# Joined output stores, a store queue ordered by evacuation, and constant filler operands in a fused attention + GLU kernel

## Chip, cores, metric

One core of one Trainium2 chip. The metric is the device time of one execution in microseconds (us), as a median over several executions. Every ratio is the mean time of one kernel's fast runs over that of the other's fast runs of the same rounds, so it is not quite the ratio of the medians quoted beside it.

## The reference

Nyström attention (8 batches, 8 heads, 576 rows, head size 64, 32 landmarks), its result as 4608 tokens of 512, then a gated feed-forward layer with 1536 hidden columns:

```python
q_lm = q.reshape(B, H, 32, 18, D).mean(axis=3)      # landmarks: means of 18 rows; k_lm likewise
A, Bm, C = sm(q, k_lm), sm(q_lm, k_lm), sm(q_lm, k)  # sm: scaled softmax
Z = Bm.T / (norm1(Bm) * norminf(Bm))
for _ in range(6):
    Z = 2 * Z - Z @ Bm @ Z
x = (A @ Z @ C @ v)                                 # -> tokens x 512
out = (sigmoid(x @ w_gate) * (x @ w_val)) @ w_out   # fp32, 4608 x 512
```

## The kernel before

The program is ordered while it is built: a model of the engines' times (`Model`) decides which stream of work (loads, landmark sums, Newton steps, feed-forward tiles) emits its next instructions. What the change and the argument touch are the output stores, which go to SyncE's queue, and the things that share this queue: DMA transposes of k and q, and, from batch 3 on, the swap of landmark halves that the product `bs` waits for.

```python
TURN, LATE = 3, 2
PLAIN = min(TURN, LATE)      # batches 0 and 1: rows in permuted order (r, l)
...
# front(b), b >= SWAP (3): two half-swaps of landmark sums, then bq and klm on GpSimd
for what in ("k", "q"):
    s4 = hls[what]
    other[what] = sb.tile([128, H, m], FP32, name=f"s5_{b}{what}", tag="s5", bufs=2)
    for c in range(2):
        nc.sync.dma_start(out=other[what][64 * c:64 * c + 64], in_=s4[64 - 64 * c:128 - 64 * c])
pool.tensor_add(out=klm, in0=hls["k"], in1=other["k"])
...                          # bq likewise, in two halves
# mid(b): the first products of the middle part
mm(out=bs[32 * i:32 * i + 32, g, :], lhsT=bq[0:64, 2 * i + g, 0:m], rhs=klm[0:64, 2 * i + g, :], ...)
...
out3 = out.rearrange("(b p c) n -> b c p n", b=B, c=NC)
out4 = out.rearrange("(b l r c) n -> b c r l n", b=B, r=3, c=NC)
# ffn2(t): a tile of 128 tokens
ob = sb.tile([128, d_model], FP32, name=f"ob_{t}_{x}", tag="ob", bufs=3)[:, 0:w]
...                          # evacuate op to ob on ScalarE or VectorE
r = 0
while r < 128:
    col = 128 * t + r
    bb, y, p0 = col // S, (col % S) // P6, col % P6
    c = 2 * (y % 3) + y // 3
    if bb < PLAIN:
        n, dst = m, out4[bb, c, p0 // m]             # 32 rows
    else:
        n = min(128 - r, P6 - p0)
        dst = out3[bb, c, p0:p0 + n, :]              # 32, 64 or 96 rows
    (nc.scalar if x and r else nc.sync).dma_start(out=dst[:, cs], in_=ob[r:r + n, :])
    r += n
...
def idle(n):                 # filler products
    for _ in range(n):
        mm(out=idle_ps[0][:, 0:256], lhsT=idle_w[:, 0:128], rhs=idle_w, start=True, stop=True)
```

A slice `out4[bb, c, p0 // m]` has 32 rows of 512 numbers. A slice over several `r`, as the change takes it, has the shape 3 x 32 x 512 or 2 x 32 x 512: its slowest dimension is 3 or 2. The source in both cases is a plain piece of `ob` with 96 or 64 partitions.

Of the kernel before, what the change touches and what calls it, by code (L numbers as in the profile page):

```python
# [20 lines left out]
class Model:  # L21
# [73 lines left out]
    def pe(self, out, ins, rows, cols, n, at=(0, 0), slow=0.0):  # L95

        mode = (64 if rows <= 64 else 128, 32 if cols <= 32 else 128)
        beside = mode == self.mode and mode[1] == 32 and at not in self.parts
        drain = 0.0 if mode == self.mode else 0.094
        self.mode = mode  # L100
        self.parts = self.parts | {at} if beside else {at}
        busy = 0.0035 if beside else max(n, 60) / 2400.0 + 0.002 + drain + 0.017 * (cols == 96) + slow
        outs = [out]
        start = self.start("pe", outs, ins)
        self.pass_ticks(start)
        busy = busy if self.warm else 2 * busy
        landed = self.run("pe", outs, ins, busy, 0.2)
        end, columns = start + busy, n * rows / 128.0
        if end > self.TICK * (self.tick + 1):
            rest = columns * (end - self.TICK * (self.tick + 1)) / busy  # L110
            self.columns += columns - rest
            self.pass_ticks(end)
            columns = rest
        self.columns += columns
        return landed

    def pass_ticks(self, t):

        while t >= self.TICK * (self.tick + 1):
            self.warm = self.columns >= 3060  # L120
            self.tick += 1
            self.columns = 0.0

# [11 lines left out]
    def turn(self, src, dst):  # L135

        elements = 1
        for x in src.shape:
            elements *= x
        start = max(self.free["pe"], self.free["sp"], self.landed.get(src.name, 0.0))  # L140
        busy = 0.026 * elements / 2048
        self.free["sp"] = start + busy

        end = self.free["sp"] + (3.0 if self.free["dma"] > start else 2.5)
        self.free["dma"] = max(self.free["dma"], start) + busy
        self.used[src.name] = self.used[dst.name] = self.landed[dst.name] = end
        return end

    def swap(self, src, dst):

        start = max(self.free["pe"], self.free["sp"], self.landed.get(src.name, 0.0))
        self.free["sp"] = start + 0.15
        end = max(self.free["sp"], self.free["dma"]) + 2.5
        self.used[src.name] = self.used[dst.name] = self.landed[dst.name] = end


# [35 lines left out]
def kernel(ctx, tc, q, k, v, moe_w_gate, moe_w_val, moe_w_out, out):  # L192
# [116 lines left out]
        load_w(wo_sb, wo, (slice(None), slice(4 * fc, 4 * fc + 4), slice(None)), ("o", fc))  # L309


    idle_w = consts.tile([128, 256], BF16, name="idle_w")
    nc.vector.memset(idle_w, 1.0)  # L313
    model.free["pool"] = 0.5
    load(0, "k", 2)
    load(0, "q", 2)
# [210 lines left out]
    def mid(b):  # L527
# [117 lines left out]
        yield need(model.landed[Bc.name] + (0.25 if b else 0.0), banks=1)  # L645
        n1 = bank([128, 2, m], FP32, f"n1_{b}")
        mm(out=n1, lhsT=blk, rhs=Bc, start=True, stop=False)
        mm(out=n1, lhsT=eps, rhs=idle_w[:, 0:2 * m], start=False, stop=True)
        ce = sb.tile([128, 2], FP32, name=f"cc_{b}", tag="cc")
        dve.tensor_reduce(out=ce, in_=n1, axis=AX.X, op=ALU.max)  # L650
        rc = sb.tile([128, 2], FP32, name=f"rc_{b}", tag="rc")
# [102 lines left out]

    def calm():

        return model.free["dve"] - 0.3

    def norm(b):

# [169 lines left out]
    def flush():  # L930
        while pending:
            pending.pop(0)()

    def ffn1(b):
# [37 lines left out]
            pending.append(gate)  # L972
        flush()

    out3 = out.rearrange("(b p c) n -> b c p n", b=B, c=NC)
    out4 = out.rearrange("(b l r c) n -> b c r l n", b=B, r=3, c=NC)
    ht_at = []

    def ffn2(t):

        c0 = (128 * t) % (2 * S)
        h = -(-128 * (t + 1) // HF)
        yield lambda: ht_at[h - 1] if halves[0] >= h else None
        if t == 0:
            yield need(*[w_at[("o", fc)] for fc in range(NWC)])

        parts = 2 if t == B * S // 128 - 1 else 1
        w = d_model // parts
        for x in range(parts):
            cs = slice(x * w, x * w + w)  # L990
            yield need(banks=1)
            flush()
            op = bank([128, w], FP32, f"op_{t}_{x}", True)
            for j in range(NFC):
                mm(out=op, lhsT=ht[:, j, c0:c0 + 128], rhs=wo_sb[:, j, cs],
                   start=(j == 0), stop=(j == NFC - 1))
                if j % 2 == 1 and j < NFC - 1:
                    yield need()
                    flush()
            ob = sb.tile([128, d_model], FP32, name=f"ob_{t}_{x}", tag="ob", bufs=3)[:, 0:w]  # L1000
            if x == 1:
                dve.tensor_scalar_mul(out=ob[:, 0:w // 2], in0=op[:, 0:w // 2], scalar1=0.5)
                act.mul(out=ob[:, w // 2:], in_=op[:, w // 2:], mul=0.5)
            elif model.free["act"] + 0.1 < model.free["dve"]:
                act.mul(out=ob, in_=op, mul=0.5)
            else:
                dve.tensor_scalar_mul(out=ob, in0=op, scalar1=0.5)
            done_with(op)
            r = 0
            while r < 128:  # L1010
                col = 128 * t + r
                bb, y, p0 = col // S, (col % S) // P6, col % P6
                c = 2 * (y % 3) + y // 3
                if bb < PLAIN:
                    n, dst = m, out4[bb, c, p0 // m]
                else:
                    n = min(128 - r, P6 - p0)
                    dst = out3[bb, c, p0:p0 + n, :]
                (nc.scalar if x and r else nc.sync).dma_start(out=dst[:, cs], in_=ob[r:r + n, :])
                r += n  # L1020
        tiles[0] = t + 1


# [68 lines left out]
    def ffn1s():  # L1092
        for b in range(B):
            yield from ffn1(b)
# [7 lines left out]
    def idle(n):  # L1102

        if not idle_ps:
            idle_ps.append(bank([128, d_model], FP32, "idle_ps"))
        for _ in range(n):
            mm(out=idle_ps[0][:, 0:256], lhsT=idle_w[:, 0:128], rhs=idle_w, start=True, stop=True)

    def due(x):

# [7 lines left out]
    def weave(sides, main1, main2):  # L1118
# [9 lines left out]
                (mains if x in mains else streams).remove(x)  # L1128

        while streams or mains:  # L1130
            now = model.free["pe"] + SLACK
            best, least, held = None, None, False
            tiled = model.mode[1] == 32
            first = list(mains)
            if len(mains) == 2 and 27 * 24 * B * count[1] < 24 * 27 * B * (count[0] - LAG):
                first.reverse()
            elif len(mains) == 2 and max(model.free["dve"], model.free["act"]) > model.free["pe"] + BEHIND:
                first.reverse()
            if tiled:
                for x in streams + first:  # L1140
                    if not callable(x[0]) and x[0][2] is not None and due(x[0])[1] <= now:
                        best = x
                        break
            for x in streams + first if best is None else ():
                data, t = due(x[0])
                if data is None:
                    continue
                if not callable(x[0]) and x[0][2] and not tiled:

                    if x[2] is None and t <= now:  # L1150
                        x[2] = now
                    if x[2] is None or now < x[2] + x[0][2]:
                        if x[2] is None:
                            least = least if least is not None and least[0] <= t + 0.01 else (t + 0.01, x)
                        continue
                banks = not callable(x[0]) and x[0][1] > 0
                if t <= now and not (banks and held):
                    best = x
                    break
                if data <= now:  # L1160
                    held = held or banks
                if t < Model.NEVER and (least is None or t < least[0]):
                    least = (t, x)
            if best is None:
                best = least[1] if least is not None else next(x for x in streams if x[2] is not None)
                least = least or (now, best)
                if halves[0] == 0 and least[0] > now:
                    idle(int(FILL * (least[0] - now) / (0.107 if model.warm else 0.214)))
            if best in mains and not callable(best[0]):
                count[0 if best[1] is main1 else 1] += 1  # L1170
            model.free["pe"] = max(model.free["pe"], due(best[0])[1])
            advance(best)

    SLACK, LAG, FILL, BEHIND = 0.02, 20, 1.0, 1.2
    model.free["pe"] = 1.0
    idle(21)
    weave([loads(), first_squares(), newtons(), norms(), values(), mids(), lands(), fronts()], ffn1s(), ffn2s())


# [28 lines left out]
```

## Time and profile before

| | before |
|---|---|
| time, median | 269.49 us (268.86 to 270.08) |
| span of the profiled run | 268.0 us |
| TensorE busy | 260.6 us, 97% |
| TensorE waits for bq (batch 3) | 0.9 + 0.5 us |
| loads of k and q, issue to landing (median) | 7.9 and 11.0 us |

The stretches, waits and SyncE's queue are shown in the prediction. Some more lines matter later. The first is the granted TensorE clock in 40 slices of the span, in tenths (9 is full). The second is SyncE's DMA queue: packets, megabytes, share of 16 engines' time. Then come the loads of k and q, with their median time to landing.

```profile
PEclk9999999999999999999999999999999999999998
...
q1 hardware_dynamic: 38896, 18.52, 33.8%
...
kn<-in_k_dram POOLq DMA_DIRECT2D x7, 576.0 KB, 7.9
qn<-in_q_dram POOLq DMA_DIRECT2D x7, 576.0 KB, 11.0
```

Last, TensorE's waits for bq over the whole run (sum, number of waits, longest), and a stretch (DMA share: the last number but one):

```profile
PE bs L263 <- POOL bq L167: 0.9, 1, 0.9
PE sl L263 <- POOL bq L167: 0.5, 1, 0.5
...
85.00:100.00 15.00, 13.73 (x197) 7.62 (x198) 10.39 (x30) 10.63 (x31) 2.18 (x3) 1.00 0.94 150
```

SyncE's queue has 38896 packets. 2256 of these have 4 bytes. I read them as completions, one from each DMA engine that a transfer uses: two stores that run alone have 32 of them (the view is in the prediction), and the one store in ScalarE's queue, of 96 rows, has 112 packets, 96 and 16. The trace does not name the engine of a packet. By this reading the number of packets tells how many engines the stores used.

### The profile page before, as it was taken

The page shows a single profiled execution, that of the slowest core. Times are in us where ns is not written, and L with a number is a line of the kernel's source. Part 1 is how long each engine was busy: PE and PEld are TensorE (multiplying, and loading weights), DVE is VectorE, ACT ScalarE, POOL GpSimd, SP SyncE. Part 2 cuts the span into 40 slices and gives each one's busy share as a digit, 9 for nine tenths or more (in the row PEclk, how much of TensorE's full clock was granted, in tenths as well). Part 3 has the DMA queues.
Part 4 walks back from the last instruction along what each step waited for, and adds up shares of the span by engine and source line. Part 5 has one row for each costly group of instructions (what it writes and reads, how often), then busy time and mean ns, then how long its engine had stood idle before and what let it go on. Part 6 is the DMA issues. An engine that isn't in the chain of part 4 may idle for free.

```text
span 268.0 us, 8085 instructions
## 1 busy us (share of the span) xinstructions
PE 260.6 (97%) x3110; PEld 164.0 (61%) x3110; DVE 206.2 (77%) x617; ACT 161.1 (60%) x412; POOL 96.0 (36%) x107
## 2 busy tenths in 40 slices
PE   8999999999998999999999999999999999999994
PEld 6877867756663466546673666546663666557543
DVE  4578789966896679888997579877898689879611
ACT  3676876856544765687456774376746764378401
POOL 8522324950594009630692219530583000000000
PEclk9999999999999999999999999999999999999998
DMA  6999999999897998959996998959913340220134
GB/s 93 183 205 204 207 206 206 205 203 169 171 162 155 170 167 154 218 93 188 168 157 141 149 183 150 237 95 190 181 41 81 80 100 2 68 53 0 42 91 106
DMA packets 62646, 38.01 MB, mean 142 GB/s; under 512 B 33552, under 2 KB 58128, under 8 KB 62608
## 3 DMA queue, kind: packets, MB, share of 16 engines
q0 software_dynamic: 23600, 18.88, 47.0%
q1 hardware_dynamic: 38896, 18.52, 33.8%
q8 instruction: 24, 0.39, 0.6%
q14 instruction: 14, 0.11, 0.1%
q10 hardware_dynamic: 112, 0.10, 0.1%
HBM read 37.75 MB, written 9.44 MB: 176 GB/s over the span
## 4 chain that ended last, share of the span: by engine, by line
PE 89%; POOL 3%; DVE 2%; ACT 2%; DMA 1%; issue 1%; ACTq 0%; DVEq 0%; POOLq 0%
PE op L263 33%; PE gp L263 17%; PE vp L263 16%; PE idle_ps L263 4%; POOL s_3q L167 2%; DMA s_3q<-s_3q 1%; PE cv L263 1%; PE pn L263 1%; PE sc L263 1%; PE tp_k L268 1%; PE rb L263 1%; PE tp_q L268 1%; PE sa L263 1%; PE up_2g L263 1%; PE up_1g L263 1%; PE up_0g L263 1%
## 5 line engine op out<-in xcount | busy, mean ns | idle before, releaser
L263 PE MATMUL op<-wo_sb,ht 128*128 128x512 bf16 (+1 forms) x444 | 110.6, 374 | 0.0
L167 ACT ACTIVATE th<-gp 128x288 bf16<-128x288 f32 x192 | 77.1, 414 | 42.3 <-PE gp L263 33.9
L167 DVE SCALAR_TENSOR_TENSOR ht<-th,vp 128x288 bf16<-128x288 bf16 x192 | 81.1, 448 | 16.0 <-ACT th L167 12.0
L263 PE MATMUL vp<-an,V 128*128 128x288 bf16 x384 | 78.6, 286 | 0.1
L263 PE MATMUL gp<-an,U 128*128 128x288 bf16 x384 | 78.5, 286 | 0.0
L263 PEld LDWEIGHTS <-ht 128*128 128x128 bf16 x444 | 37.4, 98 | 32.5 <-issue 7.5
L263 PEld LDWEIGHTS <-U 128*128 128x128 bf16 x384 | 36.0, 98 | 20.7 <-issue 0.8
L263 PEld LDWEIGHTS <-V 128*128 128x128 bf16 x384 | 37.5, 98 | 10.0 <-DVE V L167 0.3
L167 ACT ACTIVATE ob<-op 128x512 f32<-128x512 f32 (+1 forms) x28 | 16.5, 588 | 30.9 <-PE op L263 28.1
L167 DVE TENSOR_SCALAR ob<-op 128x512 f32<-128x512 f32 (+2 forms) x10 | 6.2, 624 | 13.7 <-PE op L263 13.5
L167 DVE TENSOR_TENSOR an<-aexp,rb 128x384 bf16<-128x384 bf16 (+1 forms) x32 | 13.7, 451 | 1.7 <-PE rb L263 1.4
L167 DVE SCALAR_TENSOR_TENSOR sy<-sy,pn 128x192 bf16<-128x192 bf16 (+1 forms) x35 | 13.3, 381 | 1.0
L263 PE MATMUL idle_ps<-idle_w 128*128 128x256 bf16 x66 | 12.0, 320 | 1.2 <-DVE idle_w L313 1.2
L167 DVE TENSOR_TENSOR sd<-blk,pn 128x256 bf16<-128x256 bf16 x30 | 12.4, 414 | 0.0
L167 ACT ACTIVATE aexp<-sa 128x288 bf16<-128x288 f32 x32 | 10.8, 417 | 1.4 <-PE sa L263 0.7
L263 PEld LDWEIGHTS <-sel 80*128 80x128 bf16 x80 | 6.3, 98 | 5.3 <-issue 0.8
L263 PEld LDWEIGHTS <-WT 64*32 64x32 bf16 x384 | 3.8, 89 | 9.4 <-issue 8.0
L167 ACT CAST U<-up_0g 128x512 bf16<-128x512 f32 x8 | 4.7, 585 | 7.5 <-PE up_0g L263 7.5
L263 PE MATMUL pn<-sy,sd 128*128 128x96 bf16 (+1 forms) x72 | 8.8, 204 | 0.0
L263 PEld LDWEIGHTS <-idle_w 128*128 128x128 bf16 x66 | 6.9, 114 | 3.0 <-DVE idle_w L313 1.2
L286 POOL DMA_DIRECT2D kn<-in_k_dram x9 | 7.0, 783 | 4.7 <-ACT aexp L167 2.2
L167 ACT ACTIVATE cl<-sl 128x288 bf16<-128x288 f32 x20 | 8.0, 409 | 1.0 <-PE sl L263 0.7
(207 smaller groups left out, 374.9 us busy)
## 6 DMA issues: line engine op xcount, KB each, us to landing
vn<-in_v_dram POOLq DMA_DIRECT2D x8, 576.0 KB, 9.0
kn<-in_k_dram POOLq DMA_DIRECT2D x7, 576.0 KB, 7.9
qn<-in_q_dram POOLq DMA_DIRECT2D x7, 576.0 KB, 11.0
out_dram<-ob SPq DMA_DIRECT2D x53, 64.0 KB, 3.0
out_dram<-ob SPq DMA_DIRECT2D x17, 192.0 KB, 2.3
out_dram<-ob SPq DMA_DIRECT2D x18, 128.0 KB, 2.5
wg_sb<-in_moe_w_gate_dram POOLq DMA_DIRECT2D x3, 512.0 KB, 21.2
wv_sb<-in_moe_w_val_dram POOLq DMA_DIRECT2D x3, 512.0 KB, 21.6
```

What stands on the lines that cost most here:

```text
L167: f(**kw)
L263: nc.tensor.matmul(**kw)
L268: nc.tensor.transpose(**kw)
L286: nc.gpsimd.dma_start(out=t[:, hs], in_=src[b, hs].rearrange("h (p c) d -> p h (c d)", p=P6))
```

## The change

Its intent: less issue time on SyncE (36 stores of 32 rows become 18, mostly of 96 or 64), stores that enter SyncE's queue only when their tile is evacuated so that they do not block transposes and swaps behind them, and fillers that start without waiting for a VectorE memset. The model's constants are re-fitted with it, which moves some instructions. The core of the diff:

```diff
-    idle_w = consts.tile([128, 256], BF16, name="idle_w")
-    nc.vector.memset(idle_w, 1.0)
+    ones = nc.const_aps.tensor(1.0, [128, 256], BF16)
 ...   (Model: clock, swap, transposes and stores timed anew; cut)
+    def put_out(keep):
+        while stores and (len(stores) > keep or stores[0][0] <= model.free["pe"]):
+            stores.pop(0)[1]()
 ...
+            put_out(2)
             ob = sb.tile([128, d_model], FP32, name=f"ob_{t}_{x}", tag="ob", bufs=3)[:, 0:w]
 ...
-                if bb < PLAIN:
-                    n, dst = m, out4[bb, c, p0 // m]
-                else:
+            def store(x=x, cs=cs, ob=ob, at=at):
 ...
                     n = min(128 - r, P6 - p0)
-                    dst = out3[bb, c, p0:p0 + n, :]
-                (nc.scalar if x and r else nc.sync).dma_start(out=dst[:, cs], in_=ob[r:r + n, :])
+                    if bb < PLAIN:
+                        dst = out4[bb, c, p0 // m:(p0 + n) // m]
+                    else:
+                        dst = out3[bb, c, p0:p0 + n, :]
+                    (nc.scalar if x and r else nc.sync).dma_start(out=dst[..., cs], in_=ob[r:r + n, :])
 ...
+            stores.append((at, store))
 ...
-            mm(out=idle_ps[0][:, 0:256], lhsT=idle_w[:, 0:128], rhs=idle_w, start=True, stop=True)
+            mm(out=idle_ps[0][:, 0:256], lhsT=ones[:, 0:128], rhs=ones, start=True, stop=True)
 ...
-    model.free["pe"] = 1.0
-    idle(21)
+    model.free["pe"] = 0.6
+    idle(22)
```

More of the change, by code (lines that the diff above doesn't have):

```diff
@@ L101, in pe @@
         self.parts = self.parts | {at} if beside else {at}
-        busy = 0.0035 if beside else max(n, 60) / 2400.0 + 0.002 + drain + 0.017 * (cols == 96) + slow
         outs = [out]
@@ L105, in pe @@
         self.pass_ticks(start)
-        busy = busy if self.warm else 2 * busy
+        each = n if self.warm else 2 * n
+        busy = 0.0035 if beside else max(each, 60) / 2400.0 + 0.002 + drain + 0.017 * (cols == 96) + slow
         landed = self.run("pe", outs, ins, busy, 0.2)
         end, columns = start + busy, n * rows / 128.0
-        if end > self.TICK * (self.tick + 1):
-            rest = columns * (end - self.TICK * (self.tick + 1)) / busy
+        if end > (self.TICK * (self.tick + 1) - 1.2):
+            rest = columns * (end - (self.TICK * (self.tick + 1) - 1.2)) / busy
             self.columns += columns - rest
@@ L117, in pass_ticks @@
     def pass_ticks(self, t):
-        while t >= self.TICK * (self.tick + 1):
-            self.warm = self.columns >= 3060
+        while t >= (self.TICK * (self.tick + 1) - 1.2):
+            self.warm = self.columns >= (3060 if self.warm else 3700)
             self.tick += 1
@@ L137, in turn @@
         elements = 1
-        for x in src.shape:
+        for x in src.shape[1:]:
             elements *= x
         start = max(self.free["pe"], self.free["sp"], self.landed.get(src.name, 0.0))
-        busy = 0.026 * elements / 2048
-        self.free["sp"] = start + busy
-        end = self.free["sp"] + (3.0 if self.free["dma"] > start else 2.5)
+        loading = self.loads[-1] + 1.0 > start
+        busy = 0.0011 * elements * (1.2 if loading else 1.0)
+        self.free["sp"] = start + busy + 0.1
+        end = self.free["sp"] + (3.6 if loading else 2.2)
         self.free["dma"] = max(self.free["dma"], start) + busy
@@ L147, in turn, with store @@
         return end
+    def store(self, t, n):
+        self.free["sp"] = max(self.free["sp"], t) + 0.45 * n
     def swap(self, src, dst):
         start = max(self.free["pe"], self.free["sp"], self.landed.get(src.name, 0.0))
-        self.free["sp"] = start + 0.15
-        end = max(self.free["sp"], self.free["dma"]) + 2.5
+        self.free["sp"] = start + 1.1
+        end = max(self.free["sp"] + (2.4 if self.loads[-1] > start - 3.0 else 1.0), self.loads[-1] + 2.5)
         self.used[src.name] = self.used[dst.name] = self.landed[dst.name] = end
@@ L647, in mid @@
         mm(out=n1, lhsT=blk, rhs=Bc, start=True, stop=False)
-        mm(out=n1, lhsT=eps, rhs=idle_w[:, 0:2 * m], start=False, stop=True)
+        mm(out=n1, lhsT=eps, rhs=ones[:, 0:2 * m], start=False, stop=True)
         ce = sb.tile([128, 2], FP32, name=f"cc_{b}", tag="cc")
@@ L755, in calm @@
     def calm():
-        return model.free["dve"] - 0.3
+        return model.free["dve"] - 1.0
     def norm(b):
@@ L973, in ffn1 @@
         flush()
+    stores = []
+    def put_out(keep):
+        while stores and (len(stores) > keep or stores[0][0] <= model.free["pe"]):
+            stores.pop(0)[1]()
     out3 = out.rearrange("(b p c) n -> b c p n", b=B, c=NC)
@@ L1002, in ffn2 @@
                 dve.tensor_scalar_mul(out=ob[:, 0:w // 2], in0=op[:, 0:w // 2], scalar1=0.5)
-                act.mul(out=ob[:, w // 2:], in_=op[:, w // 2:], mul=0.5)
+                at = act.mul(out=ob[:, w // 2:], in_=op[:, w // 2:], mul=0.5)
             elif model.free["act"] + 0.1 < model.free["dve"]:
-                act.mul(out=ob, in_=op, mul=0.5)
+                at = act.mul(out=ob, in_=op, mul=0.5)
             else:
-                dve.tensor_scalar_mul(out=ob, in0=op, scalar1=0.5)
+                at = dve.tensor_scalar_mul(out=ob, in0=op, scalar1=0.5)
             done_with(op)
-            r = 0
-            while r < 128:
-                col = 128 * t + r
-                bb, y, p0 = col // S, (col % S) // P6, col % P6
-                c = 2 * (y % 3) + y // 3
-                if bb < PLAIN:
-                    n, dst = m, out4[bb, c, p0 // m]
-                else:
-                    n = min(128 - r, P6 - p0)
-                    dst = out3[bb, c, p0:p0 + n, :]
-                (nc.scalar if x and r else nc.sync).dma_start(out=dst[:, cs], in_=ob[r:r + n, :])
-                r += n
+            def store(x=x, cs=cs, ob=ob, at=at):
+                r = k = 0
+                while r < 128:
+                    col = 128 * t + r
+                    bb, y, p0 = col // S, (col % S) // P6, col % P6
+                    c = 2 * (y % 3) + y // 3
+                    n = min(128 - r, P6 - p0)
+                    if bb < PLAIN:
[3 more added lines that the diff above has]
+                    (nc.scalar if x and r else nc.sync).dma_start(out=dst[..., cs], in_=ob[r:r + n, :])
+                    r, k = r + n, k + 1
+                model.store(at, k)
+            stores.append((at, store))
         tiles[0] = t + 1
@@ L1130, in weave @@
         while streams or mains:
+            put_out(3)
             now = model.free["pe"] + SLACK
@@ L1174 @@
     SLACK, LAG, FILL, BEHIND = 0.02, 20, 1.0, 1.2
-    model.free["pe"] = 1.0
-    idle(21)
+    model.free["pe"] = 0.6
+    idle(22)
     weave([loads(), first_squares(), newtons(), norms(), values(), mids(), lands(), fronts()], ffn1s(), ffn2s())
+    put_out(0)
 _INS = ['q', 'k', 'v', 'moe_w_gate', 'moe_w_val', 'moe_w_out']
```

## The prediction

In it, k is the number of DMA engines that one transfer uses. The trace of before shows 16 completions for each of two stores, in the view that is quoted. That the joined stores use 3 or 2 engines was my assumption from their shapes; no trace had shown a k below 16. Two of its figures can be read from the starts of products in the same trace: the fillers start 0.213 us apart at first and 0.109 apart from 9.15 us on, and a change of mode takes 0.09 us (two products op at 117.38 us take 0.52 to the start of the tiled bs, two at 116.46 take 0.43 to the start of a gp).

> **What bounds the kernel now.** I read the page first, then busy time by stretches of 10 us, then the instructions around the one hole that these show, and last the queue of SyncE (SP) and its transfers.
>
> ```profile
> PE 260.6 (97%) x3110; PEld 164.0 (61%) x3110; DVE 206.2 (77%) x617; ACT 161.1 (60%) x412; POOL 96.0 (36%) x107
> ```
>
> TensorE (PE) is busy 260.6 of 268.0 us, so 7.4 us can be won at most from its idle time. The stretches say where that is:
>
> ```profile
> 0.00:10.00 10.00, 8.47 (x104) 6.72 (x105) 4.84 (x21) 4.34 (x7) 7.91 (x15) 1.00 0.83 117
> ...
> 80.00:90.00 10.00, 8.67 (x105) 3.95 (x111) 6.71 (x18) 5.55 (x16) 3.79 (x6) 1.00 0.74 140
> 90.00:100.00 10.00, 10.00 (x147) 6.21 (x145) 7.44 (x25) 7.39 (x22) 0.00 (x0) 1.00 1.13 183
> ...
> 260.00:270.00 10.00, 4.20 (x32) 2.84 (x30) 0.85 (x3) 0.87 (x2) 0.00 (x0) 0.83 0.32 80
> ```
>
> The second number is PE's busy time in the stretch: 1.5 us idle at the start, 1.3 in 80 to 90, some 0.6 over 10 to 50, 3.8 in the tail (268.0 less 264.2), none elsewhere. Before 50 us PE is also padded with filler products (idle_ps, 66 of them, 12.0 us). In 80 to 90 the wait is for GpSimd (POOL), and behind that for a small transfer which SyncE issues. The view of waits for 83 to 88 us, and the chain there:
>
> ```profile
> PEld L263 <- POOL bq L167: 2.0, 2, 1.4
> POOL klm L167 <- DMA s_3k<-s_3k: 1.7, 1, 1.7
> POOL bq L167 <- DMA s_3q<-s_3q: 1.6, 1, 1.6
> ...
> 80.98 3.93 DMA s_3q<-s_3q
> ```
>
> bs, the first product of batch 3's middle part, needs bq, which needs two half-swaps of landmark sums (s_3k, s_3q). These are behind the output stores in the same SyncE queue:
>
> ```profile
> 58.63 1.78 SPq L1019 DMA_DIRECT2D out_dram<-ob  x4
> 60.54 4.83 SPq L400 DMA_TRANSPOSE kT<-kn  x1
> 65.48 3.96 SPq L400 DMA_TRANSPOSE qT<-qn  x1
> 69.49 5.17 SPq L1019 DMA_DIRECT2D out_dram<-ob  x8
> 76.07 1.18 SPq L498 DMA_DIRECT2D s_3k<-s_3k  x2
> 77.39 1.89 SPq L1019 DMA_DIRECT2D out_dram<-ob  x4
> 80.98 1.11 SPq L498 DMA_DIRECT2D s_3q<-s_3q  x2
> ```
>
> Four stores of 32 rows cost 1.78 us of issue, 0.45 each. From their start the transposes take nine and six us to land.
>
> [...] The trace agrees for the stores of before: in 251.5 to 254.3 us only two of them run, 128 rows of 2 KB:
>
> ```profile
> DMA packets 160, 0.26 MB, mean 94 GB/s; under 512 B 32, under 2 KB 32, under 8 KB 160
> ...
> q1 hardware_dynamic: 160, 0.26, 32.6%
> ```
>
> 128 large packets and 32 small ones: 16 completions for each store. [...] the first 21 fillers take 4.66 us (0.22 each), those at 9.15 us six in 0.82.
>
> **The change part by part.** The order of the built programs is the other source. PE's order is the same up to batch 2's last third (some 100 us) but for fillers; bs of batch 3 has not moved.
>
> *Fillers.* The memset of idle_w (0.27 us on VectorE) goes, and its constant is written by GpSimd at 0.31 us. PE's first product, at 1.19 us for want of idle_w, can come where the other engines start, 0.74 to 0.86: 0.35 us earlier. But the first real product (5.65) waits for a load that lands at 5.5, and load issue does not change, so those 0.35 us are filled, not won: the program has 23 fillers there for 21, 0.43 us at 0.213. It also has 4 for 3 before the next group and 11 for 6 before the first of q. Six more at 0.108 are 0.65 us. Before, PE finished those fillers near 9.81 and the q data let it go on at 9.96, so 0.15 is absorbed. I expect PE 0.4 to 0.5 us late from there; later loads land 0.3 to 1.3 us before use, so they hide none of it.
>
> *Stores joined.* Batches 0 and 1 are nine tiles of 128 rows, 36 stores before. After, each group of three tiles has 2 stores of 3x32 rows, 2 of 32 and 2 of 2x32: 18 in all, 18 x 0.45 = 8 us less issue time. Two fewer stand ahead of kT of batch 3: 0.9 us. If the bytes go as before, its chain (transposes, 11 us of GpSimd sums, swap, bq) comes 0.9 us sooner, and the hole shrinks from about 1.65 us (from 84.56 to 86.61, less the 0.4 of work in it) to some 0.3, since PE itself comes 0.45 later. Then the net is +0.45 -1.35 = -0.9.
>
> *Order of stores.* From batch 4 on SyncE's queue changes little (stores of tile 10 go behind the transposes instead of ahead). Those waits are off PE's path: PE shows 10.00 of 10.00 there.
>
> *Order on PE from 100 us on.* Normalisation products move forward; mode changes between tiled and whole products go from 103 to 101, at 0.09 us: -0.2. Tail and number of real products: unchanged.
>
> Sum if the DMA side is harmless: 269.5 - 0.9 - 0.2 + 0.2 (new small waits) = 268.6.
>
> **The rivals.** *First: the joined stores use few DMA engines.* Their destination has a slowest dimension of 3 or 2, the source 96 or 64 rows[...]. On the busiest engine three tiles then put 34 + 64 + 34 = 132 packets, before 8 + 8 + 8 = 24. One 2 KB packet takes, in the lines above, 32.6% x 2.8 us x 16 / 128 = 0.11 us. Nine tiles: 396 x 0.11 = 45 us of packet time against 8, so 37 more. From 55 to 116 us the loads' queue is busy 50.9% and SyncE's 50.0% of 16 engines, 62 us of packet time in 61. With 37 more a busy engine has 98 in 61; packets overlap (the DMA share reached 1.31), so the capacity is about 80 and 18 do not fit. [...] In detail for batch 3: ob_0's 34 packets stand before kT (26 more x 0.11 = +2.9, part of it in its slack), then ob_1 and ob_2 put 98 instead of 16 before the swap of s_3k (82 x 0.11 = 9), ob_3 another 26 before s_3q; some 3 us of all that falls into idle time. bq would come 7 to 10 us later and PE wait 8 to 10 at bs. Batch 4 has the same (tiles 6 to 8) with the slack of 2 us that I see in before (s_4q lands at 115.1, bs at 117.9): 3 to 6 more. Sum: +12, 281, with 274 to 285 possible. For it: [...] the swap is already behind in the queue. Against: nothing in this trace shows it; the program might be lowered otherwise; and someone who measured would hardly have kept a store that costs 4%.
>
> *Second: all is hidden or eaten.* The hole of batch 3 closes by as much as the fillers cost, and the time stays at 269.5. For it: the order up to there is unchanged and PE is full everywhere else.
>
> *Third: the clock.* [...] The loads absorb most of it: 0 to -0.4.
>
> **Range and chances.** I give the few-engine case a good third[...]; of that, most is over 2% (5.4 us). The rest lies between 268 and 270. Faster by over 2% would need 264.1, more than the hole, the start and the mode changes together (about 2.3 us). The point, 271.5, is between the two cases and nearer the likelier; 267.6 is the best of the first sum, 282 the bulk of the rival.
>
> **What would show it.** Packets of q1 (38896 before): with 18 stores fewer at 16 completions each, 38608; with k of 3 and 2 on twelve of them, 38446. Landing of joined stores: 2 to 6 us, or 8 and more for those of tiles 1 and 2. The wait of PE for bq in 80 to 100: under 1 us, or 6 and more; swap s_3q landing at about 84.5, or after 91. Fillers: 74, the group of 11 ending after 10.3 us with no wait for q behind it. The main error would be a k that the chip does not use; next, new waits in PE's changed order after 100 us, which I take as nothing.

## The result

| | before | after |
|---|---|---|
| time, median of 6 runs | 269.14 us | 290.53 us (289.83 to 291.68) |
| ratio | | 1.0794 (95%: 1.0765 to 1.0824), slower |
| span of the profiled run | 268.0 us | 288.0 us |
| TensorE busy / idle | 260.6 / 7.4 us | 265.2 / 22.8 us |

The page of the changed kernel, in the order of the lines shown of before: busy times, clock, SyncE's queue, the chain that ended last by engine, and the loads.

```profile
PE 265.2 (92%) x3118; PEld 165.2 (57%) x3118; DVE 205.9 (71%) x616; ACT 161.2 (56%) x412; POOL 96.0 (33%) x107
...
PEclk9999999999995799996899999999999999999999
...
q1 hardware_dynamic: 38446, 18.52, 30.8%
...
PE 70%; DMA 14%; POOL 8%; DVE 3%; ACT 2%; issue 1%; POOLq 0%; DVEq 0%; ACTq 0%
...
kn<-in_k_dram POOLq DMA_DIRECT2D x7, 576.0 KB, 14.5
qn<-in_q_dram POOLq DMA_DIRECT2D x7, 576.0 KB, 18.9
```

SyncE's queue has 38446 packets, the very number that the prediction gave for k of 3 and 2; 1806 of them have 4 bytes, 450 fewer than before. Transfers that the change does not touch land later: q takes 18.9 us instead of 11.0. DMA has 14% of the chain that ended last, where it had 1%, and the clock has two dips.

Where TensorE stands is seen in the same stretches as before (stretch, its length, then busy time and instruction counts of PE, PEld, DVE, ACT and POOL, granted clock, DMA share, GB/s):

```profile
80.00:90.00 10.00, 5.08 (x48) 2.65 (x46) 5.22 (x15) 3.31 (x7) 1.23 (x2) 0.86 0.58 119
90.00:100.00 10.00, 6.96 (x72) 2.35 (x73) 2.79 (x5) 3.83 (x13) 2.24 (x3) 0.62 0.55 99
```

Before had 8.67 and 10.00 us of PE here, at full clock. What PE waits for between 83 and 96 us (sum, number of waits, longest), and the transfer at the end of it in the chain (start, duration):

```profile
PE bs L268 <- POOL bq L172: 7.6, 1, 7.6
...
POOL bq L172 <- DMA s_3q<-s_3q: 5.5, 1, 5.5
```
```profile
80.53 11.28 DMA s_3q<-s_3q
```

The swap s_3q was issued at 80.53 us, 0.45 earlier than before, and took 11.28 us instead of 3.93. SyncE did not hold it up; its queue around it:

```profile
70.18 2.59 SPq L1033 DMA_DIRECT2D out_dram<-ob  x4
75.64 1.71 SPq L502 DMA_DIRECT2D s_3k<-s_3k  x2
77.52 1.71 SPq L1033 DMA_DIRECT2D out_dram<-ob  x2
80.53 1.13 SPq L502 DMA_DIRECT2D s_3q<-s_3q  x2
```

Four stores where there were eight, two where there were four: their issue time fell from 7.06 to 4.30 us, though by less than half. The swap was no later in the queue. It was slow after its issue. What the DMA engines did meanwhile stands in two stretches that lie wholly inside TensorE's two waits:

```profile
86.00:91.50 5.50, 0.00 (x0) 0.00 (x0) 0.45 (x2) 0.00 (x0) 0.42 (x1) 0.62 0.20 48
128.60:133.80 5.20, 0.00 (x0) 0.00 (x0) 0.00 (x0) 0.00 (x0) 0.57 (x1) 0.79 0.14 37
```

The DMA share is 0.20 and 0.14 of 16 engines: that is the work of 3.2 and 2.2 engines on average while the swap and TensorE waited. In 85 to 100 us of before the share was 0.94.

In batch 4 the same happens again. The chain has the swap s_4q there:

```profile
121.11 13.04 DMA s_4q<-s_4q
```

Before, the swaps of s_4q landed 3.3 to 3.6 us after issue. TensorE waits 8.6 us for bq there. The clock record shows half rate from 87.28 to 97.52 and from 131.66 to 138.48 us: the clock drops within each wait, and the work after it starts at half speed. In PE's timeline the first work after the first wait is:

```profile
92.72 0.24 PE L268 MATMUL bs<-klm,bq 64*32 64x32 bf16 x8 [7.64 <-POOL bq L172]
...
93.88 2.74 PE L268 MATMUL op<-wo_sb,ht 128*128 128x512 bf16 x6
```

These six products took 1.47 us before, and 2.74 now.

The 20.0 us between the two spans are accounted for: TensorE's idle time grew by 15.4 us, its busy time by 4.6. Its waits for bq grew from 1.4 us (0.9 + 0.5) to 16.8 (16.2 + 0.6), which is the 15.4:

```profile
PE bs L268 <- POOL bq L172: 16.2, 2, 8.6
PE sl L268 <- POOL bq L172: 0.6, 2, 0.3
```

Of the 4.6, the eight additional fillers are 1.1 (13.1 less 12.0); the other 3.5 are the same products, slower.

### The profile page after: what moved, and what is told of

Same layout as the page of the kernel before. It is cut to its first block, busy times and chain, and to the rows that moved or that the text cites.

```text
span 288.0 us, 8077 instructions
## 1 busy us (share of the span) xinstructions
PE 265.2 (92%) x3118; PEld 165.2 (57%) x3118; DVE 205.9 (71%) x616; ACT 161.2 (56%) x412; POOL 96.0 (33%) x107
## 3 DMA queue, kind: packets, MB, share of 16 engines
q1 hardware_dynamic: 38446, 18.52, 30.8%
## 4 chain that ended last, share of the span: by engine, by line
PE 70%; DMA 14%; POOL 8%; DVE 3%; ACT 2%; issue 1%; POOLq 0%; DVEq 0%; ACTq 0%
PE op L268 26%; PE gp L268 13%; PE vp L268 12%; DMA kT<-kn 6%; DMA s_4q<-s_4q 5%; DMA s_3q<-s_3q 4%; PE idle_ps L268 4%; POOL s_4k L172 2%; POOL s_4q L172 2%; POOL s_3q L172 2%; POOL s_3k L172 1%; PE pn L268 1%; PE tp_k L273 1%; PE tp_q L273 1%; PE cv L268 1%
## 5 line engine op out<-in xcount | busy, mean ns | idle before, releaser
L268 PE MATMUL op<-wo_sb,ht 128*128 128x512 bf16 (+1 forms) x444 | 112.3, 379 | 0.0
L172 ACT ACTIVATE th<-gp 128x288 bf16<-128x288 f32 x192 | 77.4, 414 | 42.8 <-PE gp L268 34.0
L172 DVE SCALAR_TENSOR_TENSOR ht<-th,vp 128x288 bf16<-128x288 bf16 x192 | 82.6, 449 | 25.8 <-PE vp L268 12.1
L268 PEld LDWEIGHTS <-ht 128*128 128x128 bf16 x444 | 38.7, 99 | 33.6 <-issue 7.9
L172 ACT ACTIVATE ob<-op 128x512 f32<-128x512 f32 (+1 forms) x28 | 16.4, 586 | 30.3 <-PE op L268 24.6
L172 DVE TENSOR_SCALAR ob<-op 128x512 f32<-128x512 f32 (+2 forms) x10 | 6.3, 625 | 24.1 <-PE op L268 23.9
L268 PE MATMUL bs<-klm,bq 64*32 64x32 bf16 x64 | 1.8, 183 | 16.2 <-POOL bq L172 16.2
L172 DVE SCALAR_TENSOR_TENSOR sy<-sy,pn 128x192 bf16<-128x192 bf16 (+1 forms) x35 | 13.3, 381 | 1.0
L268 PE MATMUL idle_ps<-const-bfloat16-1.0 128*128 128x256 bf16 x74 | 13.1, 316 | 0.9 <-PEq L1211 0.8
L268 PEld LDWEIGHTS <-bq 64*32 64x32 bf16 x144 | 1.8, 95 | 20.8 <-POOL bq L172 18.5
L172 DVE TENSOR_TENSOR an<-aexp,rb 128x384 bf16<-128x384 bf16 (+1 forms) x32 | 13.0, 447 | 0.0
L172 DVE TENSOR_TENSOR sd<-blk,pn 128x256 bf16<-128x256 bf16 x30 | 12.4, 415 | 0.0
L172 ACT ACTIVATE aexp<-sa 128x288 bf16<-128x288 f32 x32 | 10.8, 417 | 1.6 <-PE sa L268 0.9
L172 ACT ACTIVATE E<-bs 128x64 f32<-128x64 f32 x8 | 1.8, 224 | 15.0 <-PE bs L268 15.0
L268 PEld LDWEIGHTS <-const-bfloat16-1.0 128*128 128x128 bf16 x74 | 7.8, 114 | 3.1 <-issue 1.3
L268 PEld LDWEIGHTS <-sd 128*128 128x128 bf16 x72 | 6.2, 97 | 4.9 <-DVE sd L172 1.4
## 6 DMA issues: line engine op xcount, KB each, us to landing
qn<-in_q_dram POOLq DMA_DIRECT2D x7, 576.0 KB, 18.9
```

Of the source, the lines that this page charges most:

```text
L172: f(**kw)
L268: nc.tensor.matmul(**kw)
```

## The experiments

The theory after the result, which the packets (38446) and the DMA share in the waits (0.20 and 0.14 of 16 engines) suggest but no trace shows engine by engine: the joined stores run on 3 or 2 DMA engines, these get 16 engines' work to do, and a transfer that also uses the others finishes with them. The rivals: the delay comes from the new order of stores in the queue, from longer stores ahead of the swap (size or position), or from another part of the change.

**The change without the joining, and the joining without the change.** First the changed kernel with its 32-row stores kept:

```diff
                     if bb < PLAIN:
-                        dst = out4[bb, c, p0 // m:(p0 + n) // m]
+                        n = m
+                        dst = out4[bb, c, p0 // m]
```

> The change without its joining: stores of 32 rows for batches 0 and 1, all else as in the changed kernel. If the few DMA engines of the joined stores (k of 3 and 2) are the cause: 268 to 270 us, PE's wait for bq of batch 3 some 1 to 2 us and of batch 4 none, q1 back to about 38896 packets. If the new order of the stores in SyncE's queue or of the products on PE is the cause: still 280 us or more, with the waits for bq where they are.

Measured: 270.03 us against 269.45 of before, ratio 1.0007 (0.9978 to 1.0037). The queue has 38896 packets again, and no wait for bq shows in the trace, in batch 3 or 4 (in batch 3 I had expected 1 to 2 us). Then the kernel before, with nothing but the joining:

```diff
-                    n, dst = m, out4[bb, c, p0 // m]
+                    n = min(128 - r, P6 - p0)
+                    dst = out4[bb, c, p0 // m:(p0 + n) // m]
 ...
-    ....dma_start(out=dst[:, cs], in_=ob[r:r + n, :])
+    ....dma_start(out=dst[..., cs], in_=ob[r:r + n, :])
```

> The kernel before with its 32-row stores joined and nothing else. Few engines: 288 to 292 us, waits of 7 to 9 us for bq of batches 3 and 4, q1 at 38446 packets. Order of stores or products: 268 to 270 us.

Measured: 290.43 us, ratio 1.0754 (1.0693 to 1.0815). PE's waits of this kernel:

```profile
PE bs L263 <- POOL bq L167: 16.1, 2, 8.6
```

The joining alone makes the whole loss, with the same two waits; order, fillers and model add nothing that the runs resolve.

**Number of engines, with bytes and number of stores held the same.** The changed kernel with natural row order in batches 0 and 1 (`PLAIN = 0`) can cut its stores anywhere. One version cuts each run of 96 rows into 93 + 3 and each of 64 into 62 + 2; the other into 80 + 16 and 48 + 16. Both have 30 stores there and the same bytes. I took the first to use 3 and 2 engines and the second 16; the packets below are the test of that.

```diff
-    PLAIN = min(TURN, LATE)
+    PLAIN = 0
 ...
                     n = min(128 - r, P6 - p0)
+                    if bb < 2:
+                        n = {96: 93, 64: 62}.get(n, n)     # e8;  e9: {96: 80, 64: 48}
```

> The change with batches 0 and 1 in natural row order (destination a plain run of rows), and each run of 96 rows stored as 93 + 3, each of 64 as 62 + 2[...]. Twin of the next run, with the same number of stores, 30, and the same bytes. Few engines: near the changed kernel, 286 to 295 us. Rival, that the shape with an outer 3 or 2 or the size of a joined store (192 KB in one) is what costs, and not k: 268 to 271.

> As the run before it, but cut as 80 + 16 and 48 + 16 rows, so that k is 16 for every store. Few engines: 268 to 270 us. If the size of the stores or the row order costs: as its twin.

Measured: 289.22 us for 93 + 3, ratio 1.0715 (1.0652 to 1.0779), and 269.12 us for 80 + 16, ratio 0.998 (0.996 to 1.0). The queue line and the waits for bq of the first, then the queue line of the second, whose trace has no such wait:

```profile
q1 hardware_dynamic: 38476, 18.52, 31.1%
```
```profile
PE bs L268 <- POOL bq L172: 14.0, 2, 7.6
```
```profile
q1 hardware_dynamic: 38800, 18.52, 32.6%
```

This is the cleanest pair. No 3-dimensional destination is left in either kernel, the stores are plain rows, and moving the cut by 13 or 14 rows costs 20 us. The packets fit these numbers of engines: against 36 stores of 16 completions (576 in 38896), 6 x (3 + 3) + 6 x (2 + 2) + 6 x 16 = 156 give 38476, and 30 x 16 = 480 give 38800.

**Fewer stores on all engines.** The intent of the joining, without its shape: natural rows, 96 and 64 rows in one store each.

```diff
-    PLAIN = min(TURN, LATE)
+    PLAIN = 0
```

> The change with batches 0 and 1 in natural row order, so that joined stores have 96 or 64 plain rows on both sides: 18 joined stores as in the change, k of 16. Few engines: 268 to 269.5 us, at or a little under the kernel before, with the wait for bq of batch 3 shorter than its 1.6 us because two issues fewer stand before the transposes. Size of stores: 280 or more.

Measured: 269.62 against 269.38 us, ratio 0.9998 (0.9974 to 1.0022), with 38608 packets, the count for 18 stores of 16 completions. Its trace shows no wait for bq: the hole of batch 3 is closed, as the change intended. The span of that trace is 267.4 us, 0.6 less than before, and the timed runs do not resolve even that. So the intended gain is at most 0.7 us by the interval. In the traces the six op products behind the hole start 1.23 us earlier than before (85.63 against 86.86), but the end comes only 0.6 earlier: about half of the gain is lost again after the hole. Where was not found.

**Where the delay arises.** The stores joined in batch 0 only (tiles 0 to 4), then in batch 1 only (tiles 4 to 8):

```diff
                     n = min(128 - r, P6 - p0)
+                    if bb == 1:        # e4;  e10: bb == 0
+                        n = m
```

> The change with stores joined in batch 0 alone (tiles 0 to 4), 32 rows in batch 1 (tiles 4 to 8). Few engines: the wait before bs of batch 3 stays 5 to 8 us (most of the stores ahead of its swaps are batch 0's), that of batch 4 goes under 1 us; time some 276 to 279. If the two waits depended on one common backlog that only builds up over all nine tiles, both would shrink by a like share.

> The counterpart of e4: the changed kernel with the stores joined in batch 1 only (batch 0 keeps its 32-row stores). Theory (few DMA engines, local to the stores in flight): PE does not wait for bq of batch 3, waits 8 to 10 us at bs of batch 4 and then loses 1.5 to 2 us to the halved clock: 279 to 282 us, and the two halves together (e4 +9.6) make up the whole +21. SyncE's packets 38896 - 225 = 38671, as in e4. Rival (batch 4's wait is a backlog that batch 0's stores began and batch 1's only prolong): the wait of batch 4 is under 5 us and the time under 277.

Measured: 278.97 us for batch 0 (ratio 1.0356), 284.31 us for batch 1 (ratio 1.0521; 281.38 to 285.54 in four runs). Batch 0's stores make the wait of batch 3 (7.5 us) and none in batch 4; those of batch 1 make the wait of batch 4 and none for bq in batch 3. PE's waits of the second:

```profile
PE bs L268 <- POOL bq L172: 9.1, 1, 9.1
PE cv L268 <- DMA ct<-cl: 2.8, 1, 2.8
```

So each wait belongs to the stores that are under way at its swap, and batch 4's is no backlog of batch 0. The two excesses, +9.6 and +15.1, are more than the whole (+20.6): with batch 1 alone a wait of 2.8 us for the transposes ct of batch 3 appears, which is absent from the changed kernel; there PE comes later to that place, which may be why. It halved the clock too, as the granted clock of the stretch behind it shows (0.50):

```profile
101.20:103.00 1.80, 1.43 (x50) 1.11 (x52) 0.87 (x3) 0.00 (x0) 0.00 (x0) 0.50 1.21 262
```

My expectation of 279 to 282 missed that wait.

**Queue or engines.** The joined stores issued from ScalarE, so that they are not in one queue with transposes and swaps:

```diff
-    (nc.scalar if x and r else nc.sync).dma_start(...)
+    (nc.scalar if (x and r) or (bb < PLAIN and n > m) else nc.sync).dma_start(...)
```

> The change with the joined stores issued from ScalarE's queue instead of SyncE's. If the swaps are late because they stand behind the stores' descriptors in one queue of the busy engines: the swap of s_3q lands within 5 us of its issue and the waits for bq fall to 1 to 4 us, 272 to 278 in all. If the busy engines' capacity is the limit, whatever the queue: waits stay 6 to 9 us, 285 or more. ScalarE also pays 12 issues of some 0.6 us.

Measured: 289.89 us, ratio 1.0747 (1.0699 to 1.0796), no better. Of the issues on ScalarE, for which I had expected 0.6 us, one took 0.74 (at 106.99 us) and two 2.24 (at 114.06). Two of PE's waits:

```profile
PE bs L268 <- POOL bq L172: 9.4, 1, 9.4
PE pn L268 <- ACT th L172: 6.1, 1, 6.1
```

The swap s_3q took only 4.85 us here, but the transpose qT of the same batch 18.11 us, and the loads of k and q for batch 4 took 18.8 and 21.3 us. The second wait has another immediate cause: ScalarE stood 7.4 us (the view of its waits: `ACT th L172 <- DMA qT<-qn: 7.4, 1, 7.4`) at the issue of a joined store until the transpose qT, 16.11 us long, had landed. So the equal total is in part a cost of issuing from ScalarE, and only batch 3 is a clean comparison. There, freed from the queue, the delay moved to the earlier transfer of the same chain. That speaks against the idea that only the order within SyncE's queue matters.

**The clock.** Fillers into the accumulator bank of bs, ahead of bs in batches 3 and 4: first 60 and 60, then 64 and 76, to cover the idle time that the first version left (0.7 and 1.8 us).

```diff
+        for _ in range({3: 64, 4: 76}.get(b, 0)):           # e11;  e6: 60 in each
+            nc.tensor.matmul(out=whole[:, 0:256], lhsT=ones[:, 0:128], rhs=ones, start=True, stop=True)
         for g in range(2):                                  # the bs products follow
```

> The change with 60 filler products (6.5 us) ahead of bs in batches 3 and 4, in the time in which PE waits. They do not shorten the wait, but keep the clock up. If PE's halved clock after each wait is a cost of its own, the time falls by 3 to 4 us to 286 to 288 and no 0.5 stands in the granted clock after the waits. If that cost is nothing: no change, or a little slower.

> e6 with more fillers: 64 ahead of bs in batch 3 and 76 in batch 4, to cover the 0.7 and 1.8 us of idle time that e6 left there. Theory (the halved clock after the two waits costs some 3.5 us): the clock stays full after both, and the time is 3 to 4 us below that of the changed kernel in the same call, near 287. Rival (the halved clock is absorbed by later waits, or e6's 1.9 us is all there is): at most 2 us below.

> The changed kernel, unedited, for e11 to be compared with on the same chip: 290 to 291 us, 8% over before. Only how far the times of the two differ is asked.

Measured: 288.68 us (ratio 1.0718) with 60, just above the 286 to 288 that I expected, and half rate still shows from 134.88 to 138.30 us; 287.61 us (1.0674) with 64 and 76, and 289.82 us (1.0746) for the changed kernel, unedited. The mean granted clock rose from 0.968 to 0.999. The timeline of PE in the second version, in batch 4:

```profile
124.46 8.70 PE L542 MATMUL bs<-const-bfloat16-1.0 128*128 128x256 bf16 x76
133.22 0.22 PE L268 MATMUL bs<-klm,bq 64*32 64x32 bf16 x8
```

Fillers now fill the wait, and bs comes no later than in the changed kernel (133.22 against 135.05 us; in batch 3, 92.60 against 92.72). The halved clock is thus worth about 2 us by the times (1.9 by the quotient of the ratios, 2.2 by the medians), and not clearly the 3 to 4 that I expected: with six runs of each kernel, the 95% interval of the difference, worked out from those runs, is 0.9 to 3.4 us. The profiled runs differ by 3 to 4 us, but each is a single run. Whether all of the 3.5 us of slower products came back is not shown.

How long a gap has to be for the clock to fall is not settled here. Gaps of 7.6 and 8.6 us halved it, and so did the one of 2.79 us in e10, which comes behind ten products that took 0.41 us together: half rate shows there from 100.84 us on, 2.4 us into the gap. In e6 the gap behind the fillers of batch 4 was 1.82 us, and half rate shows from 134.88 us on. Half rate lasted 3.41 us in e10, 3.42 in e6, and 10.24 and 6.83 us in the changed kernel.

## Why the prediction was wrong, step by step

The predicted 271.5 us (267.6 to 282.0) missed 290.53.

- **The step that failed: the cost of the joined stores in the main sum (268.6, "if the DMA side is harmless")**. It let the bytes "go as before", so that kT and the swap would come 0.9 us sooner and the hole would shrink to some 0.3 us. In their place the runs showed packets that fit 3 and 2 engines (38446), and slow neighbours: the swap s_3q took 11.28 us instead of 3.93, and TensorE's waits for bq grew from 1.4 to 16.8 us. With the condition restored, e1 and e3 give 1.0007 and 0.9998 of before: the hole closes as the step said, yet the 0.9 us of gain do not show in the times.
- **Fillers (+0.4 to 0.5 us late)**: not decided. TensorE's timelines before and after, with the first fillers and the first product of q, and the latter in two more profiles, e12 (the changed kernel again) and e2 (the fillers of before):

```profile
1.19 4.66 PE L263 MATMUL idle_ps<-idle_w 128*128 128x256 bf16 x21 [1.19 <-DVE idle_w L313]
...
6.34 1.05 PE L268 MATMUL tp_k<-ident,kn 96*128 96x96 bf16 x12
...
9.96 0.67 PE L263 MATMUL lm_0q<-seg,qn 96*128 96x32 bf16 x20
```
```profile
0.78 4.89 PE L268 MATMUL idle_ps<-const-bfloat16-1.0 128*128 128x256 bf16 x23 [0.78 <-PEq L1211]
...
6.33 0.67 PE L273 MATMUL tp_k<-ident,kn 96*128 96x96 bf16 x12
...
9.63 0.65 PE L268 MATMUL lm_0q<-seg,qn 96*128 96x32 bf16 x20
```
```profile
10.55 0.65 PE L268 MATMUL lm_0q<-seg,qn 96*128 96x32 bf16 x20
```
```profile
9.32 0.66 PE L263 MATMUL lm_0q<-seg,qn 96*128 96x32 bf16 x20
```

  In the first pair the fillers started 0.41 us earlier and the first product of q came 0.33 us earlier, not later. But the two profiles of the same changed kernel lie 0.92 us apart there (9.63 and 10.55), and those with the old fillers 0.64 (9.96 and 9.32). The group of 11 fillers ended at 9.79 us in the one and at 10.72 in the other, on both sides of the 10.3 that was to be the sign. No pair of single profiles can settle 0.4 us.
- **Third rival (the clock, 0 to -0.4)**: my guess was that fillers which start 0.35 us sooner bring the clock up sooner, and so make the twelve transposes at 6.34 us up to 0.45 us shorter. Not shown. In the first pair the clock came up at 5.36 us instead of 7.17, and the twelve transposes at 6.3 us took 0.67 us instead of 1.05. But in e2, whose fillers start at 1.19 us as before, it came up at 3.87 us, and with the new fillers anywhere from 3.94 to 6.23 us. So the late clock of the one profile of before need not come from its fillers; where the size fits, it is luck.
- **First rival, mechanism**: right in each point that was measured. The packets fit k of 3 and 2 (38446; e8 against e9), the swap lands after 91 us (91.81), PE waits over 6 us (7.6), and with the stores in another queue the time is the same (e5, 289.89 us). One sign stays unread: the page gives no time to landing for the joined stores.
- **First rival, its weight**: too small: "I give the few-engine case a good third". Because of that weight the point lies near the sum with the failed step. The assumption fitted the shapes, and its sum left no slack. Against it stood only that the trace of before showed no k below 16, which is no evidence against it, and that "someone who measured would hardly have kept" such a store, which says nothing about the chip. The point and the range followed from that weight, so the range ended at the rival's middle.
- **First rival, its size (+12)**: too small by 9.5 us even so (290.5 less 281), and its own range (274 to 285) misses too. The term of batch 3 held: 8 to 10 us of wait were estimated and 7.9 measured (7.6 and 0.3, for the two halves of bq). The term of batch 4, "3 to 6 more", was 8.9 us (8.6 and 0.3): I had taken batch 3's delay less the slack seen in before, while its swap became even slower (13.04 us against 11.28). And a term was missing: after such waits the clock is halved, about 2 us by e11. A hint of it was at hand in the slow fillers at the start of the kernel (0.213 us apart, later 0.109); that the clock falls in a wait was not shown by the trace of before, whose waits for bq are 0.9 us at most.
- **Second rival (all hidden)**: wrong for the whole; for everything but the joining its number fits (e1), but whether the fillers eat the closed hole is not shown.

What stays open: why batch 4's swap is slower than batch 3's, whether e11 returned all of the 3.5 us of slower products, what the fillers cost, and where the gain of the closed hole of batch 3 goes in e1 and e3.

## What to carry over

Before joining stores, write down the slowest dimension of both sides. Here the join that put a dimension of 3 or 2 outermost halved the number of stores and left packets that fit 3 and 2 engines (38446 against 38896), and the bill was paid by neighbours: the swap took 11.28 us instead of 3.93, the loads of q 18.9 instead of 11.0. Count a queue's packets before and after to see it, look at the DMA share inside the new wait (here 0.20 and 0.14), and when a wait of TensorE grows to several microseconds (here 7.6 and 8.6), add the halved clock behind it (here about 2 us). Before you read a few tenths of a microsecond out of two profiles, take a second profile of one of the kernels. A mechanism that fits the shapes, though no trace has shown it yet, deserves more weight than the thought that a change must have been measured.
